# One leftover block of numerators, split over two halves of the tokens

## The chip, the cores and the metric

The kernel runs on one NeuronCore of a Trainium2 chip. The metric is the device time of one execution in microseconds (us). The core has four compute engines that this text names as the profile does: PE (TensorE, matrix products; PEld is its loading of weights, shown apart), DVE (VectorE), ACT (ScalarE) and POOL (GpSimd). SP (SyncE) issues the transfers (DMAs). Matrix products land in PSUM banks; ACT and DVE carry them from there to SBUF. A PSUM bank or an SBUF buffer that is used again makes its next writer wait for its last reader.

## The reference

Two blocks of linear attention, A and B, work on the same x (2048 tokens by 576 features, 32 heads of 18), and a gate per token mixes them:

```python
x = A_x
g = _sigmoid((x * gate_w).sum(-1, keepdims=True))
a = _A_ref(x, A_wqkv, A_wo)
b = _B_ref(x, B_wqkv, B_w_phi, B_wo)
return g * a + (1 - g) * b
```

In either block, with q, k, v = x @ wqkv in heads and a feature map phi:

```python
kv = jnp.einsum("bhsd,bhse->bhde", pk, v)
z = jnp.einsum("bhsd->bhd", pk)
num = jnp.einsum("bhqd,bhde->bhqe", pq, kv)
den = jnp.einsum("bhqd,bhd->bhq", pq, z)[..., None] + 1e-6
o = num / den
return (lambda x, *d: x.transpose(*d))(o, 0, 2, 1, 3).reshape(B, S, D) @ wo
```

A has phi(t) = elu(t) + 1 + 1e-6. B has a learned map per head: a product with w_phi (18 x 18), and the softmax of it beside the softmax of its negative, so 36 features per head. All is in float32.

## The kernel before

The first half (to about 290 us) makes k and v of both blocks, the sums kv and z, and folds the weights that can be folded: A's kv into A's output weights, B's map into B's query weights. The change lies in the last half, a loop over blocks of 256 tokens, which are two tiles of 128 (the even one, 2i, and the odd one, 2i+1). There are 16 tiles and so 8 blocks; the loop runs nine times, i = 0 to 8, because a block's outputs are made one turn after its transposes.

For each block the work is this:

- `q_units` (L1163): the query products of the next block (tiles `pq`, `tr`, `row` of the profile as results; `op`, `tail` are weights; `x`, `xp`, `xu`, `xv` are operands made of x), in the Strassen manner, and then the feature maps on DVE, ACT and POOL.
- `norm_a` (L1122) and `norm_b` (L1142): the denominators and the division by them. `norm_a` multiplies A's features by `z_a` on POOL (`row<-row,z_a`), sums them per head on DVE (`den<-row`), and POOL scales the features by the reciprocal (`row<-row,den`, in two pieces). `norm_b` multiplies B's features by `z_b`, one half on POOL and one on DVE (`row<-uw,z_b`), sums on DVE (`dd<-row`), multiplies by `rs` (`dd<-dd,rs`), adds (`den<-dd`), inverts, and scales the features by the result (`late<-uw,rs`, three pieces; on DVE from tile 4 on, on POOL before).
- `tr_units` (L1193): PE transposes a tile's rows. Four transposes (`tr<-ident,row`) give A's part, which ACT copies as the high half (`at<-tr`) and DVE subtracts to get the low half (`at<-tr,at`, fp32r pairs); eleven more (`tr<-ident,late`) give B's part `uT`.
- `num` (L1214): B's numerators. Eleven blocks b of three heads each: the transposed features `uT` (118 rows by 256 tokens) times `kb` (118 by 64), a plain float32 product whose result takes 64 PSUM rows. The blocks with even b go to rows 0 to 63, those with odd b to rows 64 to 127, so two neighbours use the two column halves of PE. Block 10 has no neighbour. The result lies in three banks: two of tile `tr` and one of `bk` (in the last two turns two of `pq` and one of `tr`). Each bank goes to `vo`: a copy on ACT (high half) and a subtraction on DVE (low half, `vo<-tr,vo`). Block 10 goes to the top 64 rows of the fourth chunk of `at` instead (`at<-bk`), a mixed chunk: its lower 64 rows are the last features of A.
- `out_units` (L1238): 27 products for each tile and column half: 9 chunks by 3 (high by high, high by low, low by high weights): `bk<-op,at`, `bk<-tail,at` and `bk<-op,vo`. The mixed chunk meets the weights `WO(s, 5)`, 64 rows for block 10 above 64 rows for A's last features.

The order of the work is not that of the code. All operations are recorded first (class `Plan`; every instruction therefore bears the line of the helper `emit`, L354, and the tile names tell them apart). A planner gives each a cost and a due time, and a list scheduling over the five engines sets the order in which each engine issues (`weigh` and `run`). Its cost for block 10 is 6 + 0.82 x 256 = 216 ns. At run time each engine goes through its list in order and waits where an operand or a buffer isn't ready.

The bank that receives the four transposes `tr<-ident,row` after `num` is one that `num` used two pieces earlier, so these transposes wait until DVE has made its first `vo<-tr,vo`.

Of the kernel before, what the change touches and what calls it, by code (L numbers as in the profile page):

```python
# [13 lines left out]
F32R = mybir.dt.float32r  # L14
AF = mybir.ActivationFunctionType
ALU = mybir.AluOpType
AX = mybir.AxisListType

P = 128
S, D, H, DH = 2048, 576, 32, 18  # L20
# [8 lines left out]
UB = 6 * DH + 10  # L29
NB = len(GRP3)  # L30
# [328 lines left out]
def tile_gated_mix(ctx, tc, xT, wAk, wAv, wBv, wAq, wkT, wqT, phi, woA, woB, out):  # L359
# [7 lines left out]
    wk = Pool(plan, "wk", ctx.enter_context(tc.tile_pool(name="wk", bufs=2)), 2)  # L367
# [4 lines left out]
    def r(ap):  # L372
        return ap.bitcast(F32)
# [27 lines left out]
    def uw_tile():  # L401
        return wk.tile([P, 2, D], F32, name="uw")
# [45 lines left out]
    kb = cst.tile([UB, NB, 64], F32, name="kb")  # L448
# [392 lines left out]
    for t in range(2):  # L841
        k, s = plain(x, 1, 2, 0, t, two_banks if t else pq_tile)
# [227 lines left out]
    def load_out(k, at):  # L1070
        t = op_tile() if k < 4 else tail_tile()
        WOt[k] = t
        plan.first = at
        if k < 3:
            SP.dma_start(r(t).rearrange("p (i s) n -> p i s n", i=2), WO_d[:, 2 * k:2 * k + 2])
        elif k == 3:
            to = r(t).rearrange("p (i s) n -> p i s n", i=2)
            SP.dma_start(to[:126], MA_d[:252].rearrange("(g p) s n -> p g s n", g=2))
            SP.dma_start(to[126:], MA_d[570:574].rearrange("(g p) s n -> p g s n", g=2))
        else:  # L1080
            SP.dma_start(r(t[:126]), MA_d[252:378])
            SP.dma_start(r(t[126:]), MA_d[574:])

    WOt = {}

    def WO(s, i):
        return WOt[i // 2][:, 2 * (i % 2) + s]
# [34 lines left out]
    def norm_a(t, f, ub):  # L1122
        zw = row_tile()[:, :D]
        G.tensor_tensor(zw, f[:, :D], z_a, op=ALU.mult)
        den = sm.tile([P, 32], F32, name="den")
        V.tensor_reduce(den, zw.rearrange("p (h d) -> p h d", d=DH), op=ALU.add, axis=AX.X)
        V.tensor_scalar(den, den, EPS, gate[:, 0, at_row(t):at_row(t) + 1], op0=ALU.add, op1=ALU.mult)
        V.reciprocal(den, den)

        f2 = row_tile()  # L1130
        blocks = f2[:, :384].rearrange("p (g c) -> p g c", g=3)
        G.tensor_tensor(blocks[:, :, :126].rearrange("p g (k d) -> p g k d", d=DH),
                        f[:, :378].rearrange("p (g k d) -> p g k d", g=3, d=DH),
                        den[:, :21].rearrange("p (g k) -> p g k", g=3)[:, :, :, None].to_broadcast([P, 3, GH, DH]), op=ALU.mult)
        G.tensor_tensor(f2[:, 384:582].rearrange("p (k d) -> p k d", d=DH), f[:, 378:D].rearrange("p (k d) -> p k d", d=DH),
                        den[:, 21:, None].to_broadcast([P, 11, DH]), op=ALU.mult)
        A.activation(blocks[:, :, 126:], f2[:, 576:582].rearrange("p (g c) -> p g c", g=3), AF.Copy)
        A.activation(ub_blocks(ub)[:, :, 108:], f2[:, 384:484].rearrange("p (b c) -> p b c", c=10), AF.Copy)
        A.activation(ub[:, UB * 10 + 72:UB * NB], f2[:, 484:530], AF.Copy)
        return f2  # L1140

    def norm_b(t, uw, rs, ub, engs):  # L1142
# [71 lines left out]
    def num(uT, at, last):  # L1214
        ath, atl = at
        oh, ol = ot = [wk.tile([P, KT, 256], F32R, name="vo") for _ in range(2)]
        if last:
            q = pq_tile()
            pms = [q[:, 0], q[:, 1], tr_tile()]
        else:  # L1220
            pms = [tr_tile(), tr_tile(), bank_tile()]
        with plan.piece():
            for b in range(NB):
                a, k = b % 2, b // 2 % 2
                PE.matmul(pms[b // 4][64 * a:64 * a + 64, 256 * k:256 * k + 256], kb[:, b, :], uT[:UB, b, :], start=True, stop=True,
                          skip_group_check=True)
        for m, p1 in enumerate(pms):
            j = 2 * m
            n = 2 if j < 4 else 1
            src = p1[:, :256 * n].rearrange("p (j n) -> p j n", n=256)  # L1230
            A.activation(oh[:, j:j + n], src, AF.Copy)
            V.tensor_tensor(ol[:, j:j + n], src, r(oh[:, j:j + n]), op=ALU.subtract)
            if n == 1:
                A.activation(ath[:64, 3], p1[:64, 256:], AF.Copy)
                V.tensor_tensor(atl[:64, 3], p1[:64, 256:], r(ath[:64, 3]), op=ALU.subtract)
        return ot

    def out_units(t, blk):  # L1238
        ath, atl = blk["at"]
        oh, ol = blk["ot"]  # L1240
        c = slice(P * (t % 2), P * (t % 2) + P)
        osb = row_tile()[:, :D]
        dst = out[P * at_row(t):P * at_row(t) + P]
        for hf in range(2):
            po = bank_tile()
            cc = slice(HB * hf, HB * hf + HB)
            srcs = [(ath, atl, m, 6 + m) for m in range(3)] + [(oh, ol, j, j) for j in range(KT)] + [(ath, atl, 3, 5)]
            st = []
            for hi, lo, j, i in srcs:
                st += [(hi[:, j, c], WO(0, i)), (hi[:, j, c], WO(1, i)), (lo[:, j, c], WO(0, i))]  # L1250
            for i, (l, w) in enumerate(st):
                PE.matmul(po[:, :HB], l, w[:, cc], start=(i == 0), stop=(i == len(st) - 1))
            A.activation(osb[:, cc], po[:, :HB], AF.Copy)
            if t >= NT - 2:
                SP.dma_start(dst[:, cc], osb[:, cc])
            if hf == 0:
                yield
        if t < NT - 2:
            SP.dma_start(dst, osb)
        yield  # L1260
# [24 lines left out]
    for i in range(NT // 2 + 1):  # L1285
        while norms:
            norms.pop(0)()
        cur, prev = blocks[i], blocks[i - 1]
        seqs = []
        if i and i <= NT // 2:  # L1290
            prev["ot"] = num(uT, prev["at"], i >= NT // 2 - 1)
        if i + 1 < NT // 2:
            x = x_fetch(pairs[i + 1])
            if i == 0:
                load_out(3, x["dma"])
                load_out(4, x["dma"])
            if i == 1:
                for k, m in enumerate((1, 4, 6)):
                    load_out(k, x["dma"][m:m + 1])
            uws = [extra_uw if i == 0 else uw_tile(), uw_tile()]  # L1300
            seqs.append((7, .7, q_units(i + 1, x, uws, row_tile)))
        ts = (2 * i + 1, 2 * i)
        if i < NT // 2:
            at = at_tile([2, 4, 256], F32R)
            cur["at"] = (at[:, 0], at[:, 1])
            seqs.append((8, 1, chain(*[tr_units(t, cur["at"], uT) for t in ts])))
        if i:
            seqs.append((4, 1, chain(*[out_units(t, prev) for t in (2 * i - 1, 2 * i - 2)])))
        merge(*seqs)
# [82 lines left out]
```

## Time and profile before

| | before |
|---|---|
| median of 3 runs | 561.29 us (561.02 to 561.9) |
| profiled execution | 562.4 us, its span 560.7 us |
| granted TensorE clock | 1.000 |
| PE / PEld busy | 551.6 us (98%) / 527.7 us (94%) |
| DVE / ACT / POOL busy | 421.8 / 288.3 / 245.8 us |
| eight times `num` | 88 products, 176 matmul records |

A row of the timeline reads: start in us from the span's start, length in us, engine, line, operation, result tile <- operand tiles, shape, count, and in brackets how long the engine had been idle and what ended that ("issue": nothing that the profile shows). Neighbouring instructions of a kind stand in one row with their count. A float32 product shows as two matmul records. Records of PE overlap, since the engine is pipelined: the spacing of starts gives the pace, and the length of one includes its passage through the array.

### The profile page before, as it was taken

How to read it: one execution, taken by the hardware profiler on the slowest of the kernel's cores; microseconds unless marked ns; L12 is line 12 of the kernel's file. 1: busy time of each engine (PE TensorE's matmuls, PEld its weight loads, DVE VectorE, ACT ScalarE, POOL GpSimd, SP SyncE). 2: the span in 40 equal slices, each digit the busy share in tenths (PEclk: the TensorE clock that was granted, in tenths of full speed). 3: DMA queues.
4: the chain of work that ended last, by engine and by line, in shares of the span. 5: the costliest groups of instructions: out<-in, count | busy, mean ns of one | idle time of the engine just before them, and what ended most of it. 6: DMA issues, size and time to landing. Idle time of an engine off the chain costs nothing.

```text
span 560.7 us, 11695 instructions
## 1 busy us (share of the span) xinstructions
PE 551.6 (98%) x4584; PEld 527.7 (94%) x4584; DVE 421.8 (75%) x673; ACT 288.3 (51%) x602; POOL 245.8 (44%) x218
## 2 busy tenths in 40 slices
PE   8999999999999999999999989999999999999997
PEld 8999999999999978999998989898999989899897
DVE  5872678843897997899889998769597795978810
ACT  6666687655645544543355645435443544535421
POOL 6575487632793523363228764214152332424200
PEclk9999999999999999999999999999999999999999
DMA  8739767976759566757759622132322314100001
GB/s 282 272 116 312 252 236 253 338 245 269 273 208 384 184 214 210 250 184 261 284 182 311 247 80 77 48 105 70 106 78 85 97 44 122 51 1 23 31 34 43
DMA packets 38625, 96.22 MB, mean 172 GB/s; under 512 B 4198, under 2 KB 7782, under 8 KB 37034
## 3 DMA queue, kind: packets, MB, share of 16 engines
q1 hardware_dynamic: 38570, 95.47, 50.2%
q8 instruction: 36, 0.59, 0.4%
q14 instruction: 19, 0.16, 0.1%
HBM read 59.64 MB, written 36.70 MB: 172 GB/s over the span
## 4 chain that ended last, share of the span: by engine, by line
PE 83%; DVE 10%; POOL 2%; ACT 2%; issue 1%; DMA 1%; SPq 0%; POOLq 0%; DVEq 0%; ACTq 0%
PE pq L354 35%; PE tr L354 25%; PE bk L354 23%; DVE row L354 3%; DVE dd L354 2%; DVE den L354 1%; DVE mm L354 1%; DVE ss L354 1%; POOL late L354 1%; POOL row L354 1%; DVE at L354 1%; DMA at<-xT 1%; DVE rs L354 1%; ACT row L354 1%; ACT uw L354 0%
## 5 line engine op out<-in xcount | busy, mean ns | idle before, releaser
L354 PE MATMUL pq<-op,x 128*128 128x288 f32 (+1 forms) x636 | 102.6, 297 | 0.0
L354 PEld LDWEIGHTS pq<-op,x 128*128 128x128 f32 x636 | 90.4, 189 | 0.9 <-issue 0.4
L354 PE MATMUL bk<-op,vo 128*128 128x288 f32 x480 | 71.0, 297 | 0.0
L354 PE MATMUL pq<-tail,x 128*128 128x288 f32 (+1 forms) x308 | 66.9, 300 | 0.0
L354 PEld LDWEIGHTS bk<-op,vo 128*128 128x128 f32 x480 | 65.8, 188 | 0.2 <-DVE vo L354 0.2
L354 PE MATMUL pq<-op,xp 128*128 128x288 f32 (+1 forms) x336 | 54.0, 297 | 0.0
L354 PE MATMUL bk<-op,at 128*128 128x288 f32 x288 | 51.3, 301 | 0.0
L354 POOL TENSOR_TENSOR row<-row,z_a 128x576 f32<-128x576 f32 x16 | 22.9, 1429 | 63.3 <-issue 35.7
L354 PEld LDWEIGHTS pq<-tail,x 128*128 128x128 f32 x308 | 49.1, 188 | 1.3 <-issue 0.6
L354 ACT ACTIVATE row<-bk 128x288 f32<-128x288 f32 x38 | 15.6, 411 | 64.4 <-PE bk L354 64.4
L354 PEld LDWEIGHTS pq<-op,xp 128*128 128x128 f32 x336 | 47.5, 188 | 0.2
L354 ACT ACTIVATE row<-row,epsc 128x576 f32<-128x576 f32 x54 | 41.9, 777 | 10.5 <-DVE row L354 9.4
L354 POOL TENSOR_TENSOR row<-row,den 128x378 f32<-128x378 f32 (+1 forms) x32 | 24.6, 789 | 47.8 <-DVE den L354 39.4
L354 DVE TENSOR_REDUCE ss<-uw 128x64 f32<-128x1152 f32 x23 | 31.0, 1350 | 18.5 <-ACT uw L354 17.9
L354 ACT ACTIVATE row<-tr 128x288 f32<-128x288 f32 (+1 forms) x74 | 30.2, 409 | 28.1 <-PE tr L354 27.2
L354 PEld LDWEIGHTS bk<-op,at 128*128 128x128 f32 x288 | 41.7, 189 | 0.4 <-issue 0.4
L354 ACT ACTIVATE uw<-uw 128x1152 f32<-128x1152 f32 x23 | 26.8, 1166 | 23.8 <-DVE uw L354 13.6
L354 POOL TENSOR_TENSOR x<-at,x 128x384 fp32r<-128x384 f32 (+2 forms) x35 | 31.3, 898 | 16.5 <-ACT x L354 14.4
L354 DVE TENSOR_TENSOR row<-row,pq 128x576 f32<-128x576 f32 (+1 forms) x30 | 22.5, 750 | 18.7 <-ACT row L354 14.3
L354 PE MATMUL tr<-op,xv 128*128 128x288 f32 (+1 forms) x204 | 33.7, 302 | 0.0
L354 ACT ACTIVATE uT<-tr 118x512 f32<-118x512 f32 (+1 forms) x48 | 25.9, 559 | 14.6 <-PE tr L354 14.5
L354 DVE TENSOR_TENSOR vo<-row,pq 128x540 f32<-128x540 f32 (+1 forms) x56 | 22.8, 449 | 11.4 <-ACT row L354 10.4
(206 smaller groups left out, 1264.3 us busy)
## 6 DMA issues: line engine op xcount, KB each, us to landing
xp<-s0x SPq DMA_DIRECT2D x12, 512.0 KB
at<-xT SPq DMA_DIRECT2D x18, 320.0 KB
x<-x1x SPq DMA_DIRECT2D x12, 384.0 KB
x<-s2x SPq DMA_DIRECT2D x12, 384.0 KB
s0x<-xp SPq DMA_DIRECT2D x8, 512.0 KB
out<-row SPq DMA_DIRECT2D x14, 288.0 KB
op<-wb SPq DMA_DIRECT2D x3, 1152.0 KB
wod<-op SPq DMA_DIRECT2D x3, 1152.0 KB
```

What stands on the lines that cost most here:

```text
L354: fn(*[a.real() if isinstance(a, View) else a for a in args], **{k: v.real() if isinstance(v, View) else v for k, v in kw.items()})
```

## The change

Block 10 becomes two products of 64 rows by 128 tokens: the first 128 tokens (the even tile) go to rows 0 to 63, the last 128 (the odd tile) to rows 64 to 127, both into columns 256 to 383 of the bank. They stand in both column halves, as the other pairs do. Each is copied by ACT and subtracted by DVE on its own (two instructions of 64x128 in place of one of 64x256).

For the odd tile the numerators now lie in the lower half of the mixed chunk, so A's last features have to lie in the upper half: POOL copies 64 columns of the normalised rows at the end of `norm_a` (`row<-row`, 128x64, for each of the 8 odd tiles), and since the transposed chunk takes columns 448 to 575, the features now stand in 448 to 511 also. The weights for this chunk are then needed with their halves exchanged: `load_swap` fetches them once, at i = 1, as a tile `st` by two DMAs of 64x1152, and the odd tiles' three products with the mixed chunk use it (`bk<-st,at`).

```diff
+    def load_swap():
+        t = WOt["swap"] = wk.tile([P, 2, D], F32R, name="st", bufs=1)
+        for a in range(2):
+            SP.dma_start(r(t[64 * a:64 * a + 64]), WO_d[64 - 64 * a:P - 64 * a, 5])
...
         A.activation(ub[:, UB * 10 + 72:UB * NB], f2[:, 484:530], AF.Copy)
+        if t % 2:
+            G.tensor_copy(f2[:, 448:512], f2[:, 512:576])
         return f2
...
-            for b in range(NB):
+            for b in range(NB - 1):
                 a, k = b % 2, b // 2 % 2
                 PE.matmul(pms[b // 4][64 * a:64 * a + 64, 256 * k:256 * k + 256], kb[:, b, :], uT[:UB, b, :], start=True, stop=True,
+                          skip_group_check=True)
+            for a in range(2):
+                PE.matmul(pms[2][64 * a:64 * a + 64, 256:384], kb[:, NB - 1, :], uT[:UB, NB - 1, P * a:P * a + P], start=True, stop=True,
                           skip_group_check=True)
...
             if n == 1:
-                A.activation(ath[:64, 3], p1[:64, 256:], AF.Copy)
-                V.tensor_tensor(atl[:64, 3], p1[:64, 256:], r(ath[:64, 3]), op=ALU.subtract)
+                for a in range(2):
+                    h, c = slice(64 * a, 64 * a + 64), slice(P * a, P * a + P)
+                    A.activation(ath[h, 3, c], p1[h, 256:384], AF.Copy)
+                    V.tensor_tensor(atl[h, 3, c], p1[h, 256:384], r(ath[h, 3, c]), op=ALU.subtract)
...
-                st += [(hi[:, j, c], WO(0, i)), (hi[:, j, c], WO(1, i)), (lo[:, j, c], WO(0, i))]
+                w0, w1 = [WOt["swap"][:, s] if i == 5 and t % 2 else WO(s, i) for s in range(2)]
+                st += [(hi[:, j, c], w0), (hi[:, j, c], w1), (lo[:, j, c], w0)]
...
                     load_out(k, x["dma"][m:m + 1])
+                load_swap()
```

The planner's cost for the new pair is 2 x (6 + 0.82 x 128) = 222 ns. From i = 2 on the engines keep their order, with the new instructions in it. On PE each `num` changes as here, at i = 1; the two rows of 64x128 are the halves:

```order
 L354 MATMUL tr<-uT,kb 64x256 x8
-L354 MATMUL bk<-uT,kb 64x256 x3
-L354 MATMUL pq<-tail,x_3718 128x288
+L354 MATMUL bk<-uT,kb 64x256 x2
+L354 MATMUL bk<-uT,kb 64x128 x2
+L354 MATMUL pq<-tail,x_3721 128x288
 L354 MATMUL pq<-op,xp 128x288 x6
```

The products before and behind `num` are the same ones (only a buffer's number differs).

On POOL a turn of the loop from i = 2 on reads like this before:

```order
L354 TENSOR_TENSOR row<-row,z_a 128x576
L354 TENSOR_TENSOR row<-row,den 128x3x126
L354 TENSOR_TENSOR row<-row,den 128x198
L354 TENSOR_TENSOR row<-uw,z_b 128x576 x2
L354 TENSOR_TENSOR row<-row,z_a 128x576
```

and like this after:

```order
L354 TENSOR_TENSOR row<-row,den 128x198
L354 TENSOR_TENSOR row<-uw,z_b 128x576 x2
L354 COPY row<-row 128x64
L354 TENSOR_TENSOR row<-row,z_a 128x576
L354 TENSOR_TENSOR row<-row,den 128x3x126
```

The new copy stands behind the two products with `z_b` and ahead of the next product with `z_a`.

At i = 1, behind the first `num`, the planner's list comes out in another order over some 25 us. On DVE, which there makes the numerators' low halves and the norms of block 2, it is this piece before:

```order
L354 TENSOR_TENSOR vo<-tr,vo 128x512 x2
L354 TENSOR_REDUCE ss<-uw 128x64
L354 RECIPROCAL rs<-ss 128x64
L354 TENSOR_TENSOR vo<-bk,vo 128x256
L354 TENSOR_TENSOR at<-tr,at 128x4x128
```

and this after:

```order
L354 TENSOR_TENSOR vo<-tr,vo 128x512
L354 TENSOR_REDUCE ss<-uw 128x64
L354 TENSOR_TENSOR vo<-tr,vo 128x512
L354 TENSOR_TENSOR row<-uw,z_b 128x576
L354 TENSOR_REDUCE dd<-row 128x32 x2
L354 RECIPROCAL rs<-ss 128x64
L354 TENSOR_TENSOR vo<-bk,vo 128x256
L354 TENSOR_TENSOR dd<-dd,rs 128x64
```

The second and third low halves come later, and `at<-tr,at` stands behind the sums of the denominators. Further on, the even tile's `z_b` product, its sums and its `dd<-dd,rs` have moved ahead of the next turn's `vo<-tr,vo` (i = 2), where they stood behind it. PE's list changes there to suit: the products with `vo` and `at` of block 0 are mixed in another order with those of `xv` and with the transposes.

At i = 0 the fourth of the odd tile's transposes `tr<-ident,row` moves two products back, since it waits for the copy:

```order
-L354 MATMUL tr<-ident,row 128x128 x4
-L354 MATMUL bk<-op,xp 128x288 x12
+L354 MATMUL tr<-ident,row 128x128 x3
+L354 MATMUL bk<-op,xp 128x288 x2
+L354 MATMUL tr<-ident,row 128x128
+L354 MATMUL bk<-op,xp 128x288 x10
```

On SP the two DMAs of `st` stand behind the load of an `x` tile and ahead of one of `xp`.

## The prediction

> **What bounds the kernel now.** I read the page's busy shares and chain first, then the numerators' products by their tile, then the timeline of one turn of the loop, engine by engine.
>
> ```profile
> PE 551.6 (98%) x4584; PEld 527.7 (94%) x4584; DVE 421.8 (75%) x673; ACT 288.3 (51%) x602; POOL 245.8 (44%) x218
> PE 83%; DVE 10%; POOL 2%; ACT 2%; issue 1%; DMA 1%; SPq 0%; POOLq 0%; DVEq 0%; ACTq 0%
> L354 PE MATMUL tr<-uT,kb x108: 379/379/430, 316.5 to 543.6; 118*64 118x256 f32 x108
> L354 PE MATMUL bk<-uT,kb x36: 379/379/379, 318.3 to 487.8; 118*64 118x256 f32 x36
> L354 PE MATMUL pq<-uT,kb x32: 379/379/430, 519.4 to 542.8; 118*64 118x256 f32 x32
> ```
>
> PE is busy nearly always and makes 83% of the chain, so a shorter product looks like a gain. But 10% of the chain is DVE, and the question is whose chain it is where `num` stands. The last three rows count 108 + 36 + 32 = 176 records, two for each of 88 products. PE around the `num` of i = 5:
>
> ```profile
> 451.35 1.95 PE L354 MATMUL tr<-uT,kb 118*64 118x256 f32 x16
> 453.13 1.03 PE L354 MATMUL bk<-uT,kb 118*64 118x256 f32 x6
> 454.08 0.57 PEld L354 LDWEIGHTS pq<-op,xu 128*128 128x128 f32 x4 [0.39 <-issue]
> 455.92 0.29 PE L354 MATMUL bk<-op,vo 128*128 128x288 f32 x1
> 456.20 0.42 PEld L354 LDWEIGHTS tr<-ident,row 128*128 128x128 f32 x4 [0.22 <-issue]
> ```
>
> DVE and POOL in the same 11 us:
>
> ```profile
> 440.46 0.76 DVE L354 SCALAR_TENSOR_TENSOR row<-row 128x576 f32<-128x576 f32 x1 [1.06 <-ACT row L354]
> 445.62 0.76 DVE L354 TENSOR_TENSOR row<-row,pq 128x576 f32<-128x576 f32 x1 [0.33 <-PE pq L354]
> 446.56 3.34 POOL L354 TENSOR_TENSOR row<-uw,z_b 128x576 f32<-128x576 f32 x2 [0.43 <-ACT uw L354]
> 449.85 0.74 DVE L354 SCALAR_TENSOR_TENSOR row<-row 128x576 f32<-128x576 f32 x1
> 450.74 1.42 POOL L354 TENSOR_TENSOR row<-row,z_a 128x576 f32<-128x576 f32 x1 [0.83 <-DVE row L354]
> 451.59 0.65 DVE L354 TENSOR_TENSOR dd<-dd,rs 128x64 f32<-128x64 f32 x1
> 452.27 0.19 DVE L354 SCALAR_TENSOR_TENSOR den<-dd 128x32 f32<-128x32 f32 x1
> 453.21 1.62 DVE L354 TENSOR_TENSOR late<-uw,rs 128x540 f32<-128x540 f32 x3
> 455.40 1.28 DVE L354 TENSOR_TENSOR vo<-tr,vo 128x512 fp32r<-128x512 f32 x2
> 456.93 0.41 DVE L354 TENSOR_TENSOR at<-bk,at 64x256 fp32r<-64x256 f32 x1
> ```
>
> DVE last waits for PE at 445.62 and then has no idle time marked until its first `vo<-tr,vo`, half of 1.28, which ends near 456.08 (0.64 after 455.40, with a little overlap of the two). The four transposes need that bank. Their weights load at 456.20, 0.12 later, after 0.22 of idle PE. The profile says "issue" there, but the wait ends with DVE. `num` (451.35 to 454.08) lies inside this stretch, beside a DVE that is doing something else. The same wait follows the other `num`s:
>
> ```profile
> 326.38 0.66 PE L354 MATMUL tr<-ident,row 128*128 128x128 f32 x4 [1.13 <-DVE vo L354]
> 353.97 0.63 PE L354 MATMUL tr<-ident,row 128*128 128x128 f32 x4 [0.67 <-DVE vo L354]
> 422.16 0.42 PEld L354 LDWEIGHTS tr<-ident,row 128*128 128x128 f32 x4 [0.22 <-issue]
> 490.23 0.31 PEld L354 LDWEIGHTS tr<-ident,row 128*128 128x128 f32 x3 [0.22 <-issue]
> 523.78 0.54 PE L354 MATMUL tr<-ident,late 128*118 128x128 f32 x3 [0.82 <-DVE at L354]
> ```
>
> So i = 1 and 2 wait 1.13 and 0.67, the middle turns 0.22 with a period of (490.23 - 422.16) / 2 = 34.03 us, and i = 7 waits 0.82 for DVE. Only the last `num`, i = 8, has no such wait behind it:
>
> ```profile
> 542.96 1.03 PE L354 MATMUL tr<-uT,kb 118*64 118x256 f32 x6
> 543.92 0.40 PE L354 MATMUL bk<-tail,at 128*128 128x288 f32 x1
> 545.84 0.40 DVE L354 TENSOR_TENSOR at<-tr,at 64x256 fp32r<-64x256 f32 x1
> 547.48 0.56 PE L354 MATMUL bk<-op,at 128*128 128x288 f32 x3
> ```
>
> **The products.** The six records of the third bank are blocks 8 and 9 side by side (two steps) and block 10 alone (two steps): four starts, three intervals. (1.03 - 0.379) / 3 = 0.217 us a step. Block 10 costs two steps, 0.43. As two halves side by side at half the tokens it costs two steps of 0.108: 0.22 less in each `num`, 8 x 0.22 = 1.74 in all if nothing waits. From below the bound is no gain: if the halves don't overlap, four steps of 0.108 are the old 0.43. I take 0.22, since blocks 8 and 9 overlap in the same row.
>
> What of it stays: behind `num` at i = 1 to 6 PE waits for a DVE that `num` doesn't feed in time to matter (ACT's copy waits for the products, DVE's turn comes over 2 us later), and at i = 7 for DVE as well. Seven of eight gains only make these waits longer: 0. The last stays: -0.22.
>
> The Trainium skill, page "TensorEngine Tiling (Array Packing)", section "Key Properties", says that different tiles of the array load weights and multiply in parallel, and that a change of the tiling mode drains it; by it the halves overlap as the pairs do, and the switch around `num`, whose 0.39 of idle loading stands above, stays. The trace of before agrees for pairs of 256 tokens.
>
> **The evacuation.** DVE's 64x256 took 0.41; two of 64x128 cost between 0.41 and 0.82, I take 0.55, so +0.14, and about as much on ACT. They stand behind the `vo` subtractions, which release PE; DVE idles 1.06 before 440.46, in the next turn of the same cycle, which covers it. At i = 8 the low half is ready at 546.24 and used at 547.48: 1.2 us of cover, so 0. If that cover were gone: 0.14 a turn, 1.1 in all.
>
> **POOL's copy.** The trace of before has no such copy. The nearest rows:
>
> ```profile
> L354 POOL MEMSET vo<- 128x38 f32 x2 | 0.3, 133 | 0.3 <-POOLq L1384 0.3
> L354 POOL TENSOR_TENSOR late<-uw,rs 128x72 f32<-128x72 f32 x3 | 0.9, 309 | 0.0
> 518.96 1.42 POOL L354 TENSOR_TENSOR row<-row,z_a 128x576 f32<-128x576 f32 x1 [0.84 <-DVE dd L354]
> 518.99 1.44 DVE L354 SCALAR_TENSOR_TENSOR den<-dd 128x32 f32<-128x32 f32 x1
> ```
>
> It costs 0.13 to 0.31; a copy of one operand is nearer the first, I take 0.2. It goes into POOL's 0.83 of idle time before 450.74, so it looks free. But DVE and POOL hinder each other: `den<-dd` takes 0.19 at 452.27 and 1.44 at 518.99, where it ends with POOL's `z_a` product; `dd<-dd,rs` at 451.59 takes 0.65 and ends at 452.24, with the `z_a` product (452.16). That product sets when DVE goes on, and the copy now stands ahead of it. DVE's `row<-row` (449.85) begins as POOL's `z_b` ends (449.90): if DVE is first, the copy runs when it is through at 450.59, ends near 450.8, and the `z_a` product starts 0.06 to 0.2 late. If the copy is first, `row<-row` is late by 0.13 to 0.31 and the product with it. Either delay reaches `vo<-tr,vo` in full, and PE. I take 0.12 a turn for i = 2 to 6, which is 5 x 0.12 = +0.6 (from 0 to 5 x 0.31 = 1.55; a gain has no way to come of it).
>
> The Trainium skill, page "SBUF — State Buffer", section "SBUF: two separate sides", says that the port pair of VectorE and GpSimd is an exclusive lock, held for a whole instruction by whichever began first, against VectorE operations with two SBUF inputs. The two lengthened rows above agree. By it the copy has to wait or be waited for, and speaks against a free copy.
>
> **The order at i = 1.** DVE makes there the second subtraction after `ss<-uw` and the even tile's `z_b` product, sums and `dd<-dd,rs` before the next `vo<-tr,vo`.
>
> ```profile
> 342.21 1.35 DVE L354 TENSOR_REDUCE ss<-uw 128x64 f32<-128x1152 f32 x1 [1.51 <-ACT uw L354]
> 344.14 1.53 DVE L354 TENSOR_TENSOR row<-uw,z_b 128x576 f32<-128x576 f32 x1
> ```
>
> The work moved ahead of 353.97 is a `z_b` product (0.74 if it goes like `row<-row` of the same width at 449.85), its sum (of the same width, so much the same again), `dd<-dd,rs`, `den<-dd` and a reciprocal (each between 0.19 and 0.3): an estimate of 2.1 us. Against it stand 1.51 of idle time and the 0.79 by which the `z_b` product at 344.14 was hindered (1.53 - 0.74): 2.1 - 1.51 - 0.79 = -0.2 at best. If half of the hindering stays, +0.2, and I take that; all of the idle time lost would be +1.3, more than the order makes likely, and -0.7 is the 0.67 that PE can win at most at 353.97. PE's list there holds the same products in another order, and behind a DVE chain that is worth 0.
>
> **The start and the transfers.** At i = 0 the fourth transpose waits for the copy, with two products moved ahead of it.
>
> ```profile
> 301.59 2.31 POOL L354 TENSOR_TENSOR late<-uw,rs 128x540 f32<-128x540 f32 x2 [1.09 <-DVE rs L354]
> 303.95 0.76 PE L354 MATMUL tr<-ident,late 128*118 128x128 f32 x5 [0.65 <-POOL late L354]
> 276.00:284.00 8.00, 8.00 (x76) 7.84 (x76) 5.80 (x8) 2.55 (x7) 2.30 (x2) 1.00 0.55 181
> ```
>
> POOL is idle 1.09 before `late`, so the copy fits, and PE has 0.65 to give: 0. The two DMAs of `st` are 0.59 MB (2 x 64 x 1152 x 4 bytes) where the transfers ran at 181 GB/s and the queues were 0.55 busy: 3.3 us at that rate, for weights used some 50 us later. SP issues them ahead of an `xp` load; 0. If `xp` came late it would show at the turn's first products.
>
> **The sum** against the profiled execution's 562.4: -0.22 + 0.6 + 0.2 = +0.58, so 563.0. That execution was 1.1 above the median of the runs shown (561.29); against the median, 561.9. A change under 0.2%, 1.12 us, is about what a measurement of this kernel can't tell from none.
>
> **Rivals.**
>
> 1. All eight gains count: the waits of 0.22 are a cost of PE's own switch, not of DVE, and i = 1, 2 and 7 regain theirs otherwise. For it: the profile writes "issue", and PE makes 83% of the chain. Against: the 0.12 between DVE's end and the load at 456.20, and three waits that name DVE. 561.29 - 1.74 = 559.55. Chance 0.13.
> 2. The copy holds DVE up: it gets in ahead of `row<-row` each turn at the upper price, 5 x 0.31 = 1.55, - 0.22 + 0.2: 562.8, slower. It decides from 0.23 a turn (5 x 0.23 = 1.15). For it: 449.90 and 449.85 are nearly one time. Against: DVE's instruction began first in that row and ran its plain 0.74. Chance 0.17.
> 3. The order at i = 1 costs 1.3 instead of 0.2, with the copies' 0.6: 561.29 - 0.22 + 0.6 + 1.3 = 563.0, slower. For it: the wait at 353.97 is DVE's, so anything moved ahead is late in full. Against: the 1.51 that the new order can use. Chance 0.16.
> 4. The order at i = 1 wins 0.67 and the copies cost nothing, with half of the products' gain: 561.29 - 0.67 - 0.87 = 559.75. Chance 0.08.
> 5. The halves don't run side by side: the last gain goes, 562.1; inside "same".
>
> **Chances.** Faster by over 0.2%: rivals 1 and 4, 0.21. Slower: 2 and 3, 0.33. Within 0.2%: the forecast and rival 5, 0.46. Cases of both signs hold more than half; the forecast's own range is 561.0 to 562.4. The range of 8 in 10 reaches to rival 3 with a margin for its terms and leaves out the far part of rival 1: 559.7 to 563.4.
>
> **What the profile after would show.** Two records of 118x128 side by side a step of about 0.108 apart, and the next product 0.22 earlier behind `num`. The idle time before `tr<-ident,row` at i = 3 to 6 about 0.43 plus the delay, not 0.22, with the load still 0.12 after DVE's `vo<-tr,vo`. POOL's copy of 0.13 to 0.31 behind the `z_b` products, the period 34.1 to 34.2, not 34.03. The last `num` 0.22 nearer to the end. A period of 33.8 would prove rival 1, one over 34.25 rival 2; a wait at 353.97 moved by over 1 us, rival 3. I am wrong most likely in the turn of i = 1, where the lists change too much to be summed by rows.

## The result and the profile after

The change makes the kernel slower by 0.28%: the median of 22 runs is 563.1 us against 561.39, and the ratio 1.0028 (95% interval 1.0022 to 1.0035), which is 1.2 to 2.0 us. The range held the time. The likeliest case, within 0.2%, did not come: the forecast of +0.6 was about 1 us too small, and rival 3 with its 563.0 came nearest, though only a part of it is what happened.

The busy shares and the chain of the profile after, whose execution has a span of 561.4 us (before 560.7) at a granted clock of 1.000:

```profile
PE 550.3 (98%) x4600; PEld 526.7 (94%) x4600; DVE 423.8 (75%) x681; ACT 289.6 (52%) x610; POOL 251.2 (45%) x226
PE 63%; DVE 25%; ACT 4%; issue 3%; POOL 3%; DMA 1%; SPq 0%; POOLq 0%; DVEq 0%; ACTq 0%
```

PE is busy for 1.3 us less and the kernel is longer. The chain says why: DVE's share of it rose from 10% to 25%. Work was taken from the engine that looks full and waiting was added to it.

PE around the `num` of i = 5, to be read beside the same rows of before:

```profile
452.06 1.95 PE L354 MATMUL tr<-uT,kb 118*64 118x256 f32 x16
453.84 0.82 PE L354 MATMUL bk<-uT,kb 118*64 118x256 f32 x8
454.59 0.57 PEld L354 LDWEIGHTS pq<-op,xu 128*128 128x128 f32 x4 [0.17 <-issue]
456.86 0.42 PEld L354 LDWEIGHTS tr<-ident,row 128*128 128x128 f32 x4 [0.38 <-issue]
464.41 0.30 PEld L354 LDWEIGHTS pq<-tail,x 128*128 128x128 f32 x2 [0.29 <-DVE row L354]
```

The third bank now has eight records and takes 0.82 instead of 1.03, the two halves' records starting in pairs 0.109 apart (454.272 and 454.381); from the start of `num` to the next load it is 454.59 - 452.06 = 2.53 instead of 2.73. So the halves run side by side. But the idle time before the four transposes grew from 0.22 to 0.38, and 7.5 us further down stands a wait that the profile of before does not have: 0.29 for DVE's `row`.

DVE over the same stretch, after and then before. The piece at 457.70 is the one on rows 64 to 127: the profile does not show rows, but the experiment e1 below has that piece first by its code, and there it has the same spacing (0.44 behind its predecessor, 0.33 to the next).

```profile
456.06 1.28 DVE L354 TENSOR_TENSOR vo<-tr,vo 128x512 fp32r<-128x512 f32 x2
457.25 0.42 DVE L354 TENSOR_TENSOR vo<-bk,vo 128x256 fp32r<-128x256 f32 x1
457.70 0.29 DVE L354 TENSOR_TENSOR at<-bk,at 64x128 fp32r<-64x128 f32 x1
458.03 0.24 DVE L354 TENSOR_SCALAR den<-den,gate 128x32 f32<-128x32 f32 x1
458.58 0.69 DVE L354 TENSOR_TENSOR row<-uw,z_b 128x576 f32<-128x576 f32 x1
459.30 0.69 DVE L354 TENSOR_TENSOR at<-tr,at 128x512 fp32r<-128x512 f32 x1
463.60 0.75 DVE L354 TENSOR_TENSOR row<-row,pq 128x576 f32<-128x576 f32 x1
```

```profile
456.60 0.42 DVE L354 TENSOR_TENSOR vo<-bk,vo 128x256 fp32r<-128x256 f32 x1
457.26 0.23 DVE L354 TENSOR_SCALAR den<-den,gate 128x32 f32<-128x32 f32 x1
457.79 0.70 DVE L354 TENSOR_TENSOR row<-uw,z_b 128x576 f32<-128x576 f32 x1
458.40 0.68 DVE L354 TENSOR_TENSOR at<-tr,at 128x512 fp32r<-128x512 f32 x1
462.50 0.74 DVE L354 TENSOR_TENSOR row<-row,pq 128x576 f32<-128x576 f32 x1
463.44 0.30 PEld L354 LDWEIGHTS pq<-tail,x 128*128 128x128 f32 x2
```

`row<-row,pq` reads the `pq` bank into which the `pq<-tail` products go. Before, it ended at 463.24 and the load came 0.20 later without idle time: nobody waited, with next to nothing to spare. From the first `vo` to `row<-row,pq` DVE took 462.50 - 455.40 = 7.10; now it takes 463.60 - 456.06 = 7.54, and PE waits. The period went with it, from 34.03 to (491.12 - 422.58) / 2 = 34.27:

```profile
422.58 0.42 PEld L354 LDWEIGHTS tr<-ident,row 128*128 128x128 f32 x4 [0.35 <-issue]
491.12 0.42 PEld L354 LDWEIGHTS tr<-ident,row 128*128 128x128 f32 x4 [0.36 <-issue]
```

The two profiled spans differ by 0.7 only, less than the medians, because in the execution profiled after, the last half began 0.8 us earlier. A fixed point is the second load of four `tr<-ident,row` in the loop's first turn, at 307.69 before and 306.87 after. Counted from that load, the lateness against before (us) of the same later instructions, in the profiles of the kernel after and of the experiments told below:

| instruction (start before) | after | e10 | e3 | e4 | e9 | e11 | e5 | e12 | e13 |
|---|---|---|---|---|---|---|---|---|---|
| transposes, i = 1 (326.38) | 0.05 | 0.75 | -0.01 | -0.02 | -0.02 | -0.05 | 0.01 | -0.03 | 0.76 |
| transposes, i = 2 (353.94) | 1.11 | 0.96 | 0.08 | 0.07 | -0.02 | 1.00 | 0.05 | -0.93 | -0.28 |
| transposes, i = 4 (422.16) | 1.24 | 1.01 | 0.24 | 0.05 | 0.20 | 0.94 | 0.42 | -1.37 | -0.82 |
| transposes, i = 6 (490.23) | 1.71 | 1.25 | 0.58 | 0.03 | 0.68 | 0.90 | 0.85 | -1.77 | -1.67 |
| `num`, i = 8 (541.18) | 1.85 | 1.28 | 0.65 | 0.04 | 0.82 | 0.89 | 0.94 | -1.86 | -1.84 |
| last products (556.90) | 1.63 | 1.06 | 0.44 | 0.03 | 0.82 | 0.88 | 1.36 | -1.87 | -2.05 |

The column of after is the account: about +1.1 in the turn of i = 1, about 0.24 a turn from i = 3 to 6 (0.7 in all up to i = 8), and -0.22 at the last `num`. That is 1.6, what the medians show. The experiments take these three apart.

### The profile page after: what moved, and what is told of

Same layout as the page of the kernel before. It is cut to its first block, busy times and chain, and to the rows that moved or that the text cites. A ratio compares the mean times of both kernels' runs of the same rounds, so it can differ in the third digit from the quotient of the medians.

```text
span 561.4 us, 11741 instructions
## 1 busy us (share of the span) xinstructions
PE 550.3 (98%) x4600; PEld 526.7 (94%) x4600; DVE 423.8 (75%) x681; ACT 289.6 (52%) x610; POOL 251.2 (45%) x226
## 4 chain that ended last, share of the span: by engine, by line
PE 63%; DVE 25%; ACT 4%; issue 3%; POOL 3%; DMA 1%; SPq 0%; POOLq 0%; DVEq 0%; ACTq 0%
PE pq L354 27%; PE tr L354 22%; PE bk L354 14%; DVE row L354 6%; DVE den L354 4%; DVE dd L354 4%; ACT row L354 2%; DVE mm L354 2%; DVE uw L354 2%; DVE late L354 2%; DVE ss L354 1%; DVE rs L354 1%; DVE vo L354 1%; POOL late L354 1%; ACT uw L354 1%
## 5 line engine op out<-in xcount | busy, mean ns | idle before, releaser
L354 PE MATMUL bk<-op,at 128*128 128x288 f32 x240 | 42.4, 302 | 0.0
L354 PEld LDWEIGHTS bk<-op,at 128*128 128x128 f32 x240 | 34.5, 189 | 0.2 <-issue 0.2
```

The lines of the kernel that those rows point to most:

```text
L354: fn(*[a.real() if isinstance(a, View) else a for a in args], **{k: v.real() if isinstance(v, View) else v for k, v in kw.items()})
```

## The experiments

Most kernels below replay a list: the planner's order for before (or for after) is written out as numbers, every operation that both kernels have is issued in that order, and the new ones are put in at a named distance. So the order and the work can be changed one at a time. The edit is this line, with a new function that puts the operations in order, and `extra` names how many instructions of its engine a new operation stands behind:

```diff
-        order = self.order()
+        order = replay(self)
```

### The work alone, the order alone (e1, e2, e11)

e1 does the whole change in before's order (one of POOL's copies stands twice at i = 0); the piece of block 10 on the upper rows (64 to 127) is made first, the one on the lower rows five DVE instructions later.

```diff
+            extra(plan, 0)
...
         if t % 2:
             G.tensor_copy(f2[:, 448:512], f2[:, 512:576])
+            extra(plan, 0)
...
-                for a in range(2):
+                for a in (1, 0):
...
                     A.activation(ath[h, 3, c], p1[h, 256:384], AF.Copy)
+                    if a == 0:
+                        extra(plan, 0 if last else 3, 2)
                     V.tensor_tensor(atl[h, 3, c], p1[h, 256:384], r(ath[h, 3, c]), op=ALU.subtract)
+                    if a == 0:
+                        extra(plan, 0 if last else 5, 2)
```

> The whole change, but every instruction that the kernel before has stands in the order of before, the turn i = 1 included; only the new instructions are put in between. Theory A (my reading of the two traces: the new order at i = 1 costs 1.06 us, the evacuation in two pieces on DVE 0.24 us in each of the turns 3 to 6, the copy nothing, and only the last numerators keep their 0.22): the 1.06 goes and 0.6 us is left over the kernel before (0.3 to 0.9), with a period of 34.27 us in the middle turns. Theory B (POOL's copy holds DVE up): as the change, +1.6 us. Theory C (the order at i = 1 is all that costs): -0.2 us, period 34.03.

e2 does before's work in after's order, and changes nothing but the list:

> The kernel before without any part of the change, its instructions put in the order that they have in the changed kernel (which differs at i = 0 and i = 1). Theory A: the turn i = 1 ends about 1.1 us later (0.8 to 1.3), the middle turns keep 34.03 us, in all +1.1 us. Theory B: no difference, within 0.3 us.

e1 took 562.66 against 561.08 (1.0031, 1.002 to 1.0043) and e2 563.97 (1.005, 1.0036 to 1.0064). So the work in the old order costs as much as the change, and the old work in the new order costs even more; by these two runs alone the loss can't be divided. Both have a flaw. In e1 it is the copy that stands twice (e10 mends that). In e2 block 10's copy and subtraction stand where after has the second of its two pieces, and PE waits for them, which neither kernel does:

```profile
460.43 0.19 PEld L354 LDWEIGHTS bk<-op,at 128*128 128x128 f32 x1 [0.38 <-DVE at L354]
```

e11 repeats it with block 10's pair at the place of the first piece.

> The kernel before without any part of the change, its instructions in the order of the changed kernel, the copy and subtraction of block 10 now at the place of the first piece (in the earlier run of this kind they stood at the place of the second, so PE waited for them in each turn). Theory A: the turn i = 1 ends about 1.1 us later (0.8 to 1.3), the middle period stays 34.03 us, +1.1 us in all. If the order costs nothing: no difference.

It took 562.12 against 561.02 (1.0015, 1.0004 to 1.0025, which is 0.2 to 1.4 us). Its profile is 1.00 late at i = 2 and from there on it loses nothing more. So the order at i = 1 alone costs about 1 us, and the loss of the middle turns is not the order's.

Where the microsecond goes is seen on DVE. Before, after the row at 342.21 that the prediction shows:

```profile
325.63 1.29 DVE L354 TENSOR_TENSOR vo<-tr,vo 128x512 fp32r<-128x512 f32 x2 [0.20 <-POOL late L354]
353.19 1.22 DVE L354 TENSOR_TENSOR vo<-tr,vo 128x512 fp32r<-128x512 f32 x2
```

After:

```profile
324.86 0.69 DVE L354 TENSOR_TENSOR vo<-tr,vo 128x512 fp32r<-128x512 f32 x1 [0.29 <-POOL late L354]
327.33 1.76 DVE L354 TENSOR_TENSOR row<-uw,z_b 128x576 f32<-128x576 f32 x1
341.19 1.18 DVE L354 TENSOR_TENSOR row<-uw,z_b 128x576 f32<-128x576 f32 x1
353.49 1.22 DVE L354 TENSOR_TENSOR vo<-tr,vo 128x512 fp32r<-128x512 f32 x2
```

From the first `vo` of one turn to that of the next it is 353.19 - 325.63 = 27.56 before, of which 1.51 is idle, so 26.05 of work; after it is 353.49 - 324.86 = 28.63, with no idle time marked. The work between grew by 2.58, the idle time gave back 1.51, and 1.07 is left. Two of the `z_b` products in it take 1.76 and 1.18, where the one of before's 329.55 took 0.75; the first begins as POOL begins its `uw<-row,mm` (327.30, 1.17 long), the second while POOL is in a product with `den` (340.93 to 341.76).

### POOL's copy (e10, e3)

e10 is e1 with each copy once (and the two DMAs of `st` one place later on SP). e3 is e1 without the copies, so that A's last features are missing in the odd tiles' upper half.

```diff
-        if t % 2:
-            G.tensor_copy(f2[:, 448:512], f2[:, 512:576])
```

> As the first run with the whole change in the order of before, where one of POOL's copies stood twice at i = 0 and held up the transposes there by 0.8 us; now each of the eight copies stands once. If the copies cost nothing (theory A, D): as the run without the copies, +0.6 us over the kernel before (0.3 to 0.8), the middle period 34.15 to 34.2 us. If the copies are what costs (theory B): +1.5 us or more.

> As the run with the whole change in the order of before, but POOL's copies of 128x64 are left out (the odd tiles' mixed chunk then lacks A's last features in its upper half, so the odd tiles' output lacks their part). Theory A: the same time as with the copies, within 0.15 us, and a period of 34.27 us. Theory B: the period falls to 34.03 us and the time by 0.9 us or more against the run with the copies.

e10 took 562.63 against 561.02 (1.0029, 1.0018 to 1.0039), e3 561.64 against 561.08 (1.001, 1.0002 to 1.0019). The difference of about 1 us does not lie where it was expected. The table has e10 at 0.75 already at i = 1 and e3 at -0.01; from i = 4 to 6 e10 loses 0.12 a turn and e3, without a copy, 0.17. In the middle turns the copies cost nothing. At i = 0, in before's order, the first one makes a transpose wait, and in e10 PE waits once more, which it does not in e3:

```profile
299.99 0.33 PE L354 MATMUL tr<-ident,row 128*128 128x128 f32 x1 [0.75 <-POOL row L354]
314.17 1.09 PE L354 MATMUL tr<-ident,late 128*118 128x128 f32 x8 [0.56 <-POOL late L354]
```

That the table says 0.75 too is chance. The first wait lies ahead of the fixed point, and PE makes up for most of it there: from `bk<-op,xu` (297.03) to the fixed point e10 takes 10.39, before (from 297.59) 10.10, so 0.3 is lost ahead of it. The 0.75 of the table comes later: `at<-tr,at` of the delayed transposes waits 0.21 for ACT on DVE (300.98), DVE and POOL run late from there on, and PE waits for POOL's `late` at 314.17.

The planner's own order hides this: in the profile after the wait for the copy is 0.19, and there is none at the second place.

Why a copy of 0.84 is free in a middle turn, from POOL and DVE after:

```profile
L354 POOL COPY row<-row x8: 229/832/844, 299.6 to 519.1; 128x64 f32<-128x64 f32 x8
```

```profile
450.56 0.84 POOL L354 COPY row<-row 128x64 f32<-128x64 f32 x1
450.57 0.74 DVE L354 SCALAR_TENSOR_TENSOR row<-row 128x576 f32<-128x576 f32 x1
451.39 1.42 POOL L354 TENSOR_TENSOR row<-row,z_a 128x576 f32<-128x576 f32 x1
```

The copy takes 0.23 by itself and 0.83 to 0.84 in most turns: it ends (451.40) just after DVE's `row<-row` (451.31), as if it had waited for it. But the `z_a` product needs that `row<-row` anyway. It starts 0.08 after DVE's end; before, without a copy, it started 0.15 after (450.59 to 450.74). The Trainium skill, page "SBUF — State Buffer", section "SBUF: two separate sides", has the two engines lock each other out for a whole instruction where VectorE reads two inputs from SBUF. The lengths 0.23 and 0.84 agree with it. The blocked copy is free here because the next instruction on its engine waits for the same event.

### The evacuation (e4, e9, e7)

e4 is before with block 10's copy and subtraction in two pieces of 64x128, both on rows 0 to 63.

```diff
-                A.activation(ath[:64, 3], p1[:64, 256:], AF.Copy)
-                V.tensor_tensor(atl[:64, 3], p1[:64, 256:], r(ath[:64, 3]), op=ALU.subtract)
+                for a in (1, 0):
+                    c = slice(P * a, P * a + P)
+                    A.activation(ath[:64, 3, c], p1[:64, 256 + P * a:384 + P * a], AF.Copy)
...
+                    V.tensor_tensor(atl[:64, 3, c], p1[:64, 256 + P * a:384 + P * a], r(ath[:64, 3, c]), op=ALU.subtract)
```

> The kernel before in its own order, its products as they were; only the copy and the subtraction of block 10 (64x256) are made as two of 64x128 each, the second one a few instructions later, as in the changed kernel. Theory A: the period is 34.2 to 34.3 us instead of 34.03 and the time +0.9 us (0.6 to 1.1), the products before row<-row,pq on DVE being 0.2 us or more later than what PE can wait for. If DVE's idle time covers it, as I had forecast: no difference, within 0.15 us.

561.52 against 561.08 (1.0005, 0.9996 to 1.0013), and its column of the table stays at 0.03. An instruction more is not the cause: that theory fell. DVE took 461.70 - 454.66 = 7.04 to `row<-row,pq`:

```profile
454.66 1.28 DVE L354 TENSOR_TENSOR vo<-tr,vo 128x512 fp32r<-128x512 f32 x2
455.86 0.41 DVE L354 TENSOR_TENSOR vo<-bk,vo 128x256 fp32r<-128x256 f32 x1
456.19 0.27 DVE L354 TENSOR_TENSOR at<-bk,at 64x128 fp32r<-64x128 f32 x1
456.39 0.22 DVE L354 TENSOR_SCALAR den<-den,gate 128x32 f32<-128x32 f32 x1
461.70 0.75 DVE L354 TENSOR_TENSOR row<-row,pq 128x576 f32<-128x576 f32 x1
```

Against the rows of after two things differ. The second piece stands elsewhere in DVE's list (below). And the piece at 457.70 there lies on rows 64 to 127, and starts 0.45 after its predecessor, not 0.33. e9 is before with that alone: block 10's product of 256 tokens is made on rows 64 to 127 and evacuated there, in place of A's last features, which are left out; its engines keep the lists of before in full.

```diff
-                a, k = b % 2, b // 2 % 2
+                a, k = (b + b // 10) % 2, b // 2 % 2
...
-                A.activation(ath[:64, 3], p1[:64, 256:], AF.Copy)
-                V.tensor_tensor(atl[:64, 3], p1[:64, 256:], r(ath[:64, 3]), op=ALU.subtract)
+                A.activation(ath[64:, 3], p1[64:, 256:], AF.Copy)
+                V.tensor_tensor(atl[64:, 3], p1[64:, 256:], r(ath[64:, 3]), op=ALU.subtract)
```

> The kernel before in its own order, one thing changed: block 10's product of 256 tokens goes to PSUM rows 64 to 127 instead of 0 to 63, and its one copy and one subtraction (64x256) read and write rows 64 to 127; there they take the place of A's last features, whose part is so left out. Same number of instructions as before. Theory D (new: it is not the two pieces that lengthen DVE's chain but the rows: an instruction on rows 64 to 127 doesn't overlap its neighbours on DVE): from the first vo<-tr,vo to row<-row,pq DVE takes 7.3 to 7.45 us instead of 7.10, and the middle period goes to 34.1 to 34.2 us, in all +0.3 to +0.6 us. If the rows don't matter: 34.03 us and no difference.

562.07 against 561.02 (1.0023, 1.0014 to 1.0032). No instruction more, no half, no copy and before's order, and yet the loss of the middle turns is there: (0.68 - 0.20) / 2 = 0.24 a turn, as after. Its DVE, and its PE at the place of the new wait:

```profile
455.05 1.28 DVE L354 TENSOR_TENSOR vo<-tr,vo 128x512 fp32r<-128x512 f32 x2
456.24 0.41 DVE L354 TENSOR_TENSOR vo<-bk,vo 128x256 fp32r<-128x256 f32 x1
456.69 0.43 DVE L354 TENSOR_TENSOR at<-bk,at 64x256 fp32r<-64x256 f32 x1
457.15 0.24 DVE L354 TENSOR_SCALAR den<-den,gate 128x32 f32<-128x32 f32 x1
457.69 0.69 DVE L354 TENSOR_TENSOR row<-uw,z_b 128x576 f32<-128x576 f32 x1
458.42 0.69 DVE L354 TENSOR_TENSOR at<-tr,at 128x512 fp32r<-128x512 f32 x1
462.54 0.75 DVE L354 TENSOR_TENSOR row<-row,pq 128x576 f32<-128x576 f32 x1
463.34 0.30 PEld L354 LDWEIGHTS pq<-tail,x 128*128 128x128 f32 x2 [0.22 <-DVE row L354]
```

The instruction is hardly longer (0.43 for 0.41), but its neighbours no longer overlap it: 0.45 from the one ahead to it and 0.46 from it to the next, against 0.33 and 0.33 before. A third gap, from `row<-uw,z_b` to `at<-tr,at`, grew from 0.61 to 0.73. Together 0.37 of the 7.49 - 7.10 = 0.39; some 0.14 of that is what before had to spare at `pq<-tail` (0.20 from DVE's end to the load there, 0.05 here), and 0.25 is left.

e7 is e1 with the lower piece's subtraction put eight DVE instructions later.

```diff
-                        extra(plan, 0 if last else 5, 2)
+                        extra(plan, 0 if last else 13, 2)
```

> The whole change in the order of before, and the even tile's low half (the second subtraction of 64x128 on DVE) put about eight instructions later, behind row<-row,pq, the subtraction's result being needed by PE only some 10 us later. Theory A: the 0.2 us of it leaves the chain from vo<-tr,vo to row<-row,pq; the period falls from 34.27 to between 34.03 and 34.15 us, and the whole is within 0.3 us of the kernel before, at best 0.2 us under it. If the evacuation isn't what costs: as with the order of before alone.

562.82 against 561.37 (1.0023, 1.001 to 1.0035), more than the 0.3 us that was expected, with the 0.8 of i = 0 in it that e1 and e10 have. From i = 4 to 6 it loses 0.06 a turn where e10 loses 0.12. The place of the second piece is worth about that; neither of the two places undoes the loss of the first.

The place also tells why after loses 0.24 a turn where e10 loses 0.12. In the middle turns e10 has the DVE list of e4, piece for piece, only with the first piece on the upper rows, and takes 463.67 - 456.26 = 7.41 from the first `vo` to `row<-row,pq` where e4 takes 7.04. After differs from e10 there only in the second piece, which stands right behind `at<-tr,at`, and takes 7.54. So of after's 0.44 over before's 7.10 the rows are the larger part, and some 0.13 is the place of the second piece.

### Who hides the products (e5, e8, e12, e13)

e5 makes block 10 twice, in before's order.

```diff
-            for b in range(NB):
+            for b in (*range(NB), NB - 1):
```

> The kernel before in its own order, block 10's product made twice (the second writes the same values to the same place), so each of the eight numerators' groups is two steps of 0.217 us, 0.43 us, longer. If PE sets the pace everywhere: 8 x 0.43 = +3.5 us. If DVE's chain hides it as I forecast: the waits of 1.13 and 0.67 us (i = 1, 2) and 0.82 us (i = 7) take it in full, the waits of 0.22 us in the four middle turns take half, and the last group nothing: 4 x 0.21 + 0.43 = +1.3 us.

562.78 against 561.37 (1.0025, 1.0016 to 1.0034): 1.4 us for eight products of 0.43, which are 3.5. In the table a middle turn loses (0.85 - 0.42) / 2 = 0.21, half of the product's price, and only the last `num` pays 0.42. The transposes behind `num` no longer stand idle:

```profile
456.64 0.60 PE L354 MATMUL tr<-ident,row 128*128 128x128 f32 x4
```

So the 0.22 that the profile calls "issue" was time to spare behind `num`, and rival 1 is dead.

e8 does the change at the last `num` alone.

```diff
-            for b in range(NB - 1):
+            for b in range(NB - 1 if split else NB):
...
-            for a in range(2):
+            for a in range(2 if split else 0):
...
-            prev["ot"] = num(uT, prev["at"], i >= NT // 2 - 1)
+            prev["ot"] = num(uT, prev["at"], i >= NT // 2 - 1, i == NT // 2)
```

> Only the last block's numerators (i = 8) are made in two halves, with one copy for tile 15, the exchanged weights and the two-piece evacuation there; all else and the order as in the kernel before. Theory A: the one gain that no wait takes, -0.2 us (-0.3 to -0.1), without any cost; that is near what five rounds can tell. If the halves didn't run side by side: 0.

561.37 against 561.37 (0.9995, 0.9984 to 1.0006): the interval holds a gain of 0.22 us (0.9996) and none at all. Its profile has the gain, 0.28 late at the last `num` and 0.07 at the last products, behind a transfer that came late in that execution at i = 1.

```profile
311.48 1.87 PE L354 MATMUL pq<-op,xu 128*128 128x288 f32 x12 [0.64 <-DMA xu<-x0x]
```

If DVE is what PE waits for behind `num`, DVE's order is worth more than any product. e12 is before with two moves in DVE's list: the sum `den<-row` (at i = 2 with its two followers) goes behind the first `vo<-tr,vo`, and `row<-row,pq` ahead of the three `late<-uw,rs`. The first move also reaches the turn of i = 7, which the expectation leaves out. A middle turn of DVE's list differs like this (lists of instructions, not code):

```diff
-L354 TENSOR_REDUCE den<-row 128x32
-L354 TENSOR_TENSOR vo<-tr,vo 128x512 x2
+L354 TENSOR_TENSOR vo<-tr,vo 128x512
+L354 TENSOR_REDUCE den<-row 128x32
+L354 TENSOR_TENSOR vo<-tr,vo 128x512
...
-L354 TENSOR_TENSOR late<-uw,rs 128x10x54 x2
-L354 TENSOR_TENSOR late<-uw,rs 128x72
-L354 TENSOR_TENSOR row<-row,pq 128x576
+L354 TENSOR_TENSOR row<-row,pq 128x576
+L354 TENSOR_TENSOR late<-uw,rs 128x10x54 x2
+L354 TENSOR_TENSOR late<-uw,rs 128x72
```

> The kernel before, only DVE's order changed in the turns 2 to 6: the den<-row sum (in turn 2 with the two instructions behind it) stands behind the first vo<-tr,vo instead of ahead of it, and row<-row,pq stands ahead of the three late<-uw,rs instead of behind them. If PE's waits of 0.22 us in the turns 3 to 6 and of 0.67 us at 353.97 are waits for DVE, as I forecast, they go: -0.9 to -1.5 us, a period of 33.8 us. If they are a cost of PE's own switch: no difference.

559.52 against 561.35 (0.9971, 0.9959 to 0.9982): 1.6 us faster than before (1.0 to 2.3), more than was expected. The transposes load without idle time, and `row<-row,pq` comes 457.74 - 451.42 = 6.32 behind the first `vo` instead of 7.10:

```profile
451.42 0.68 DVE L354 TENSOR_TENSOR vo<-tr,vo 128x512 fp32r<-128x512 f32 x1
452.59 0.49 PEld L354 LDWEIGHTS tr<-ident,row 128*128 128x128 f32 x4
457.74 0.75 DVE L354 TENSOR_TENSOR row<-row,pq 128x576 f32<-128x576 f32 x1
```

e13 joins e12's moves to the whole change as e10 has it. Of the lines that mark what moves, these two mark the first `vo`:

```diff
+            if m == 0:
+                plan.swaps[0][0].add(plan.ops[-1].i)
```

> The same order of DVE with the whole change in the order of before. With DVE's wait out of the way the halves' 0.21 us should show in each turn that no longer waits: 0.2 us a turn less than the run without the halves in the turns 3 to 6, a period of 33.6 us, in all -0.4 to -1.0 us against that run, if DVE's longer chain doesn't become the next wait. If the halves bring no shorter product, or DVE's chain is the wait again: the same time as that run, or 0.2 to 0.5 us more.

559.74 against 561.35 (0.9977, 0.9967 to 0.9987). As a time it equals e12 and isn't 0.4 to 1.0 less, as was expected, but its column of the table is another one: it begins with 0.76 at i = 1, about what e10 has, and then gains (1.67 - 0.82) / 2 = 0.43 a turn where e12 gains 0.20. The 0.22 between them is what the prediction put on the halves, and it is now paid out in every middle turn, since no wait stands behind `num` any more. With the planner's order at i = 0 and 1 kept from costing anything, the two gains would stand together, an estimate of 0.8 below e13; that kernel wasn't tried.

## Why the prediction was right or wrong

- **The products: right.** 0.22 a `num` was forecast, and 0.20 to 0.21 measured (2.73 to 2.53; 1.03 to 0.82). The Trainium skill's rule that different tiles of the array multiply in parallel (page "TensorEngine Tiling (Array Packing)", section "Key Properties") is borne out for halves of 128 tokens too. One reading was wrong, without weight in the sum: the 0.39 of idle loading behind `num` does not stay but is 0.17 after, so 0.22 of it was the lone block 10.
- **That seven of eight gains are lost: right.** The middle turns wait 0.35 to 0.38 instead of 0.22, the turn of i = 1 waits 1.38 instead of 1.13 (below), and the last `num` keeps 0.22. The prediction named 0.43 and more for the middle turns; 0.38 and the 0.29 of the new wait for `row` are 0.67 at i = 5, which is 0.45 more than before: the 0.20 that `num` gave, and the 0.24 by which a turn grew. e5 and e13 show it from both sides: the wait swallows 0.22 of an added product, and without the wait the halves gain 0.22.

```profile
325.61 0.66 PE L354 MATMUL tr<-ident,row 128*128 128x128 f32 x4 [1.38 <-DVE vo L354]
331.21 0.40 PE L354 MATMUL bk<-op,vo 128*128 128x288 f32 x1 [1.21 <-DVE vo L354]
354.26 0.63 PE L354 MATMUL tr<-ident,row 128*128 128x128 f32 x4 [0.57 <-DVE vo L354]
```

- **The evacuation: wrong, 0 forecast, 0.24 a turn and 0.7 to 0.8 in all measured** (after and e9). The step that failed is "DVE idles 1.06 before 440.46, in the next turn of the same cycle, which covers it". It followed DVE to its next idle time and not to the next instruction that another engine waits for: `row<-row,pq` stands between, and PE's load there had some 0.14 to spare. The bound of 1.1 for a lost cover was nearer to the loss, but for another reason: two pieces cost nothing in e4, rows 64 to 127 do (e9), and in after the place of the second piece adds to it. The prediction made a period over 34.25 the proof of rival 2; the period is 34.27, and it is this that made it.
- **POOL's copy: wrong, +0.6 forecast, 0 measured in the middle turns** (e3 loses there as much as e10). The copy did get blocked and did take its 0.84. The step that failed is "Either delay reaches `vo<-tr,vo` in full": the `z_a` product behind the copy waits for the same DVE instruction as the copy. Rival 2 is dead with it.
- **The order at i = 1: the mechanism right, the size wrong, +0.2 forecast, about +1.0 measured** (e11; 1.11 at i = 2 in the profile after). The term mis-sized is the 2.1 us of moved work less half of the 0.79 of hindering: DVE's work between the two `vo` grew by 2.58, since the `z_b` products were hindered at other places, and more (1.76 and 1.18 are 1.44 over twice 0.75). The 1.51 of idle time was used up whole. PE pays at another place than the one forecast: it waits 1.21 at 331.21 for the third bank's low half, which now stands behind sums and products, and at the forecast place 0.57 (354.26) where it waited 0.67. Rival 3 had this term as 1.3 for the other reason, the idle time lost.
- **The start and the transfers: right, 0.** SP issues `st` at 283.33 and the `xp` load behind it at 284.58; no wait of PE names it, and the transposes of i = 1 are 0.05 late. That the copy fits at i = 0 holds for the planner's order alone: in before's it costs about 1 us (e10 against e3).

```profile
283.33 1.15 SPq L354 DMA_DIRECT2D st<-wod  x2
284.58 0.53 SPq L354 DMA_DIRECT2D xp<-s0x  x1
```

The forecast sum was -0.22 + 0.6 + 0.2 = +0.58; the measured one is -0.22 + 0 + 1.1 + 0.7 = +1.6, against 1.57 by the ratio. The sign and the range came out partly by luck, as a term of 0.6 that isn't there stood in for one of 0.7 that was called covered.

## What to carry to other kernels

Before a cost on a second engine is called covered, follow that engine's list to the next instruction that the busiest engine waits for, and read how long ahead of its use that one ends; the next idle time of the engine says nothing. When a planner puts out another order, add up the second engine's work between two fixed points over the whole stretch, with what hinders it, instead of the pieces that moved. And where PE is 98% busy but waits a little at the same place in every turn, try the order of the other engine first: here two moves in DVE's list won 0.3%, while the shorter product could show itself only after them.

## What the runs showed of the hardware

DVE's subtraction out of PSUM on rows 64 to 127 does not overlap its neighbours as the same one on rows 0 to 63 does: 0.12 to 0.13 more on either side (0.33 to 0.45 and 0.46 at 64x256 in e9; 0.33 to 0.45 and 0.20 to 0.33 at 64x128 after against e4). The instruction itself is about as long as before (0.43 for 0.41, 0.29 for 0.27). DVE did not wait for ACT there: ACT's copy of block 10 had ended 2.04 us earlier in e9, and 2.09 earlier before.

The third gap, from `row<-uw,z_b` to `at<-tr,at`, is 0.72 to 0.73 in the middle turns of every kernel that has a piece on rows 64 to 127 there (after, e1, e3, e7, e9, e10, e13) and 0.61 in all others. All three gaps have one form. An instruction starts 0.03 behind the end of its predecessor (0.414 long and 0.445 apart, 0.428 and 0.460, 0.693 and 0.724 in e9), where it otherwise starts some 0.08 ahead of it (0.416 and 0.331, 0.408 and 0.330, 0.696 and 0.612 before). And the three instructions are the piece on rows 64 to 127, the first one behind it that reads SBUF (`den<-den,gate`), and the first one behind it that reads PSUM (`at<-tr,at`). So these rows fit a rule by which a DVE instruction waits for its predecessor's end when it starts on other rows than the last reader of the same memory. No run varies that by itself: the rule is argued from the rows, while the cost of the upper rows is shown by e9.
